# Seven block products for eight in one more token group of a channel product, on one TensorE

## The chip, the cores and the metric

The kernel runs on one NeuronCore of a Trainium2 chip. Its engines run side by side, each through its own instruction queue: TensorE (PE, matrix products, with its weight loads PEld), VectorE (DVE), ScalarE (ACT), GpSimd (POOL) and SyncE (SP, which issues DMAs). They wait for each other only on semaphores. The metric is device time in microseconds (us) of one execution, the median of several runs.

## What is computed

Three layers one after the other on 2 x 768 tokens of 384 channels: a linear-attention recurrence, a gated MLP with a product over the tokens, and an MLP mixer. The change lies in the last product pair of the mixer:

```python
def _moe2_ref(x, w_tok1, w_tok2, w_ch1, w_ch2):
    xt = x.transpose(0, 2, 1)
    h = np.maximum(xt @ w_tok1, 0.0) @ w_tok2
    u = x + h.transpose(0, 2, 1)                    # (2, 768, 384)
    h2 = np.maximum(u @ w_ch1, 0.0) @ w_ch2         # 384 -> 1536 -> 384
    return (u + h2)
```

## The kernel before

Every product of two float32 matrices is made of three products of float32r parts: each operand is split into a high part (rounded, `h`) and a low part (`l`, the rest), and `prod` issues high x high, low x high and high x low (L270, L271, L272), all added in a bank of PSUM.

The last stage, `rest`, computes `relu(u @ w_ch1) @ w_ch2`. The 1536 tokens lie in three groups g = 0, 1, 2 of 512 (two halves of 256, `ONE` and `TWO`), the 1536 hidden channels in six blocks k of 256 (`G`), the 384 input channels in three tiles of 128. A block n = (g, k) is one step of the stage.

- The first product has two forms. The plain form, `C1` (letters a and b of the order), makes 2 x 3 x 3 = 18 products of 512 columns per block; ACT takes relu and the high part from PSUM, DVE the low parts and the differences that the second product needs (`C1a`, `C1b`, letters c and d). The form `C1s` (letters g to m) takes two of the three input tiles and both halves of the tokens as a 2 x 2 block product in seven products (Strassen in Winograd's form), with the third input tile in full: 6 products of 512 columns and 21 of 256. It writes three PSUM banks x, y, z; ACT copies z (`sz`) and a part of y; DVE adds c1 and c2 (named p1, p2) from PSUM; then come relu and high part on ACT (`C1r`, o and q), the low parts (`C1l`, p and r), and the four differences `C1t` (s) on DVE.
- `C1s` needs sums of the two token halves (`sums_of_u`, E, and `split_u`, F) and of the weights (`sums_of_c1`, C, and `split_c1`, D), made on DVE, ACT and POOL in four shared tiles `st`.
- The second product, `C2` (digits 1 to 7) and `C2d` (8, 9), is the seven-product form for all groups, with right operands split by `right_split` (e, f, t, u: th on ACT, tl on DVE, L567). Its five totals per group stay in five PSUM banks for the six blocks and are added to u and stored by `finish` (G to P) and `finish_rest` (Q, S). `residual` (R) makes u from its parts on POOL.
- `z` and `Z` test whether the fast path of the recurrence was sound: two comparisons and a sum on DVE, a 1x1 product `pf` on PE, one comparison `fi` on DVE.

Before, groups 0 and 1 are in the plain form and group 2 in the form `C1s`. What runs when is written out by hand: the string `REST` has one letter for each part, and the n-th time a letter comes it does block n of its kind. Each engine works off its instructions in the order in which the string issues them. Three PSUM banks (`ps3`) serve the first product, five (`ps5`) the totals. DVE stands between nearly everything: a bank of the first product is free for the next block once DVE has read it.

Of the kernel before, what the change touches and what calls it, by code (L numbers as in the profile page):

```python
# [7 lines left out]
F32 = mybir.dt.float32  # L8
# [5 lines left out]
ALU = mybir.AluOpType  # L14
# [3 lines left out]
B, H, S, D = 2, 8, 768, 48  # L18
E = H * D
# [4 lines left out]
DCH = 1536  # L24
# [3 lines left out]
G = 2 * P  # L28
# [41 lines left out]


REST = (
# [5 lines left out]


REBIAS = 2.0 ** -112  # L80
# [5 lines left out]
class Dense:  # L86
# [442 lines left out]

    def C1(self, n, b):  # L530

        p, (g, k) = self.mm(2 * G), divmod(n, DCH // G)
        for q in range(3):
            self.prod(p, self.C1w(k, b, q), self.u[g, q], q == 0, q == 2)
        if b == 0:
            self.raw[n] = [self.temp(q) for q in ("r", "ta", "tb")]
            self.hid[n] = []
        r, h, l = self.raw[n][0], self.big("h"), self.big("l")
        act = self.nc.scalar.activation
        act(r[:, b * G:(b + 1) * G], p[:, b * G:(b + 1) * G], AF.Relu)  # L540
        act(h, p, AF.Relu)
        self.hid[n].append((h, l))
        self.raw[n].append(p)
# [68 lines left out]

    def C1l(self, n, j):
        h, l = self.hid[n][j]
        self.nc.vector.tensor_tensor(l, self.raw[n][j], h.bitcast(F32), op=ALU.subtract)

    def C1t(self, n):
        c1, c2 = self.raw[n]
# [121 lines left out]
    def rest(self, sound=None, flag=None, look=None):  # L740

        self.top.close()
        pool = lambda n, bufs: self.ctx.enter_context(self.tc.tile_pool(name=n, bufs=bufs, reuse_waits="tile"))
        self.pbig = pool("big", 8)
        self.pbig.tile([P, BPAD], F32, name="bpad", bufs=1)
        self.ptmp = pool("tmp", 6)
        self.po = pool("o", 1)
        self.banks = [self.ps3]
        self.ws, self.sw, self.raw, self.acc, self.hid, self.rests = ({} for _ in range(6))
        self.turn = False  # L750
        n = DCH // G

        later = lambda f, *a: lambda i: f(i + 2 * n, *a)
        parts = dict(A=self.sums_of_c2, B=self.split_c2, C=self.sums_of_c1, D=self.split_c1, E=lambda i: self.sums_of_u(i + 1),
                     F=lambda i: self.split_u(i + 2), a=lambda i: self.C1(i, 0), b=lambda i: self.C1(i, 1), c=self.C1a, d=self.C1b,
                     e=lambda i: self.right_split(i, 0), f=lambda i: self.right_split(i, 1),
                     o=later(self.C1r, 0), p=later(self.C1l, 0), q=later(self.C1r, 1), r=later(self.C1l, 1),
                     s=later(self.C1t), t=later(self.right_split, 0), u=later(self.right_split, 1),
                     R=self.residual, z=lambda i: flag(sound()) if sound else None, Z=lambda i: look() if look else None)
        parts.update({q: later(self.C1s, m) for m, q in enumerate("ghijklm")})  # L760
        parts.update({str(q): lambda i, q=q: self.C2(i, q) for q in range(1, 8)})
        parts.update({q: lambda i, t=t: self.C2d(i, t) for t, q in enumerate("89")})
        parts.update({q: lambda i, m=m: self.finish(i, m) for m, q in enumerate("GHIJKLMNOP")})
        parts.update({q: lambda i, t=t: self.finish_rest(i, t) for t, q in enumerate("QS")})
        count = dict.fromkeys(parts, 0)
        for part in REST.replace(" ", ""):
            parts[part](count[part])
            count[part] += 1
# [3 lines left out]
def fast(tc, ins, out, flag_pool):  # L772
    nc = tc.nc
    with ExitStack() as ctx:
# [7 lines left out]
        with ExitStack() as c1:  # L782
# [71 lines left out]
            def masked(i, o):  # L854
                A[i, o] = t = dn.a2(nm="A").rearrange("p (h c) -> p h c", c=P)
                nc.scalar.activation(t, PA[i][o], AF.Copy)  # L856
                nc.gpsimd.affine_select(out=t, in_=t, pattern=[[0, NHP], [1, P]],  # L857
                                        compare_op=ALU.is_gt, fill=0.0, base=0,
                                        channel_multiplier=-1)
# [126 lines left out]
            def ahead(f, n):  # L986
                return lambda i: f(i + n) if i + n < N else None
# [7 lines left out]
            def fetch_rest():  # L995
# [4 lines left out]
            parts = dict(  # L1000
                L=ahead(load, 2), N=ahead(load_nat, 2), F=ahead(fwd, 1), K=ahead(decay, 1),
                U=ahead(rk, 1), q=ruk, A=a0, S=scores, e=lambda i: masked(i, 0),
# [179 lines left out]
```

## Time and profile before

| | us |
|---|---|
| median of 3 runs | 381.81 (381.11 to 382.2) |
| the profiled execution | 383.05 |
| its span, first to last instruction | 381.3 |
| last stage, first channel product to last | 232.1 to 374.8 |
| mean granted TensorE clock | 0.995 of 2.4 GHz |

The profile gives busy time for each engine, the releaser of each wait (inferred from semaphore events), and single instructions with start and duration. Durations of DVE and PE instructions overlap at their ends, so a queue's pace is read from start to start. A page shows shares over the whole span; a table by windows shows them for a stage.

### The profile page before, as it was taken

The numbers are of one execution on the slowest core, as the hardware profiler recorded it, in microseconds if no ns is written. First come the engines' busy times: TensorE is split into PE (matmuls) and PEld (weight loads), VectorE is DVE, ScalarE is ACT, GpSimd is POOL, SyncE is SP. The second block draws the span as 40 slices with busy tenths as digits, with TensorE's granted clock in tenths as the row PEclk, the third lists the DMA queues.
The fourth block names the chain that finished last, engine by engine and source line by source line (L and its number), as shares of the span: only waits on it lengthen the run. The fifth ranks groups of instructions, "written<-read, shape, count | busy, mean of one in ns | idle before, by whom it ended". The sixth has DMA issues, their size and how long they took to land.

```text
span 381.3 us, 8493 instructions
## 1 busy us (share of the span) xinstructions
PE 371.1 (97%) x3287; PEld 331.3 (87%) x3287; DVE 319.2 (84%) x566; ACT 234.3 (61%) x528; POOL 195.0 (51%) x221
## 2 busy tenths in 40 slices
PE   8899999999999999999999999999999999999993
PEld 3477788889999999999999998898888888999992
DVE  6999998889888696897879687777977997799893
ACT  3599888787345896955666766545343562564650
POOL 2235468771634557768667746888714122412101
PEclk9999999999999999999999999999999999999998
DMA  8566385373343042235552340000002000011002
GB/s 242 154 217 169 110 258 156 103 212 116 95 116 147 2 124 70 83 87 159 145 164 85 124 125 0 1 2 1 2 0 69 2 14 3 0 43 42 2 2 93
DMA packets 16449, 33.72 MB, mean 88 GB/s; under 512 B 2448, under 2 KB 6544, under 8 KB 16400
## 3 DMA queue, kind: packets, MB, share of 16 engines
q1 hardware_dynamic: 15968, 32.69, 28.2%
q8 instruction: 28, 0.46, 0.5%
q10 hardware_dynamic: 432, 0.39, 0.3%
q14 instruction: 21, 0.17, 0.2%
HBM read 30.72 MB, written 2.36 MB: 87 GB/s over the span
## 4 chain that ended last, share of the span: by engine, by line
PE 88%; DVE 4%; ACT 3%; issue 1%; DMA 1%; POOL 0%; DVEq 0%; ACTq 0%
PE mm L270 26%; PE mm L272 25%; PE mm L271 25%; PE py L893 2%; PE pa L851 2%; PE py L877 1%; DVE wf L803 1%; PE mm L836 1%; PE mm L434 1%; PE tr L295 1%; PE pkv L911 1%; PE py L887 1%; DMA wf<-in_dram 1%; DVE st L230 1%; PE pt L864 1%
## 5 line engine op out<-in xcount | busy, mean ns | idle before, releaser
L232 DVE SCALAR_TENSOR_TENSOR st<-st 128x384 int32<-128x384 int32 (+1 forms) x50 | 35.3, 705 | 1.7
L857 POOL TENSOR_SCALAR_AFFINE_SELECT A<-A 128x512 f32<-128x512 f32 x24 | 18.5, 778 | 33.5 <-ACT A L856 32.0
L230 DVE SCALAR_TENSOR_TENSOR st<-st 128x384 int32<-128x384 int32 (+1 forms) x50 | 32.8, 656 | 2.3 <-ACT st L228 2.3
L540 ACT ACTIVATE r<-mm 128x256 f32<-128x256 f32 x24 | 9.2, 382 | 39.9 <-PE mm L272 39.9
L227 ACT ACTIVATE st<-st 128x384 f32<-128x384 f32 (+1 forms) x50 | 25.7, 515 | 9.9 <-DMA st<-in_dram 8.5
L228 ACT ACTIVATE st<-st 128x384 int32<-128x384 uint32 (+1 forms) x50 | 25.7, 514 | 0.0
L829 POOL TENSOR_TENSOR rk<-kr 112x512 f32<-112x512 f32 x12 | 20.0, 1666 | 10.8 <-DMA kr<-in_dram 10.8
L380 POOL TENSOR_TENSOR vs<-vs,uT 128x384 f32<-128x384 f32 x16 | 19.6, 1231 | 7.3 <-DVE vs L378 7.2
L382 ACT ACTIVATE gh<-vs 128x384 fp32r<-128x384 f32 x16 | 8.4, 524 | 24.1 <-POOL vs L380 24.1
L682 POOL TENSOR_TENSOR o<-o,part 128x256 f32<-128x256 f32 x9 | 7.1, 802 | 31.2 <-ACT part L684 23.4
L270 PE MATMUL mm<-xt,wuh 128*128 128x256 f32 x72 | 20.8, 289 | 0.0
L803 DVE TENSOR_TENSOR_SCAN wf<-wf,scan 112x516 f32<-112x516 f32 x12 | 18.6, 1554 | 2.3 <-DMA wf<-in_dram 1.8
L271 PE MATMUL mm<-xt,wuh 128*128 128x256 f32 x72 | 20.3, 282 | 0.0
L272 PE MATMUL mm<-xt,wul 128*128 128x256 f32 x72 | 20.3, 282 | 0.0
L670 POOL TENSOR_TENSOR o<-uh,ul 128x512 f32<-128x512 f32 x9 | 12.2, 1365 | 14.7 <-DVE tb L620 10.8
L546 DVE SCALAR_TENSOR_TENSOR l<-mm,h 128x512 fp32r<-128x512 f32 x24 | 16.3, 680 | 2.5 <-PE mm L271 2.5
L817 DVE TENSOR_TENSOR_SCAN wf<-wf,scan 112x516 f32<-112x516 f32 x12 | 17.9, 1489 | 0.4
L138 PE MATMUL mm<-scan 112*128 112x512 bf16 x49 | 14.1, 428 | 3.2 <-DVE scan L944 1.7
L567 DVE TENSOR_TENSOR tl<-tb,th 128x512 fp32r<-128x512 f32 x18 | 15.3, 851 | 2.2 <-ACT th L566 2.1
L825 DVE TENSOR_TENSOR kr<-kr,wf 112x1024 f32<-112x1024 f32 x12 | 15.9, 1328 | 1.2 <-DVE wf L817 0.2
L567 DVE TENSOR_TENSOR tl<-ta,th 128x512 fp32r<-128x512 f32 x18 | 16.6, 924 | 0.3 <-issue 0.3
L270 PE MATMUL mm<-woh,gh 128*128 128x384 f32 x48 | 16.2, 337 | 0.0
(298 smaller groups left out, 1487.6 us busy)
## 6 DMA issues: line engine op xcount, KB each, us to landing
st<-in_dram SPq DMA_DIRECT2D x38, 384.0 KB, 3.4
kr<-in_dram SPq DMA_DIRECT2D x12, 448.0 KB, 4.2
st<-in_dram SPq DMA_DIRECT2D x18, 256.0 KB, 4.1
wf<-in_dram SPq DMA_DIRECT2D x12, 227.5 KB, 3.0
vn<-in_dram SPq DMA_DIRECT2D x12, 192.0 KB, 4.6
out_dram<-o SPq DMA_DIRECT2D x15, 128.0 KB, 1.7
bsg<-in_dram SPq DMA_DIRECT2D x2, 192.0 KB, 3.6
out_dram<-o ACTq DMA_DIRECT2D x3, 128.0 KB, 2.1
```

What stands on the lines that cost most here:

```text
L227: nc.scalar.activation(high.bitcast(F32), high.bitcast(F32), AF.Copy, scale=REBIAS)
L228: nc.scalar.activation(low, low.bitcast(U32), AF.Copy, scale=TOP3, bias=FLOOR)
L230: nc.vector.scalar_tensor_tensor(low, high, -2 ** 31, low, op0=ALU.bitwise_and, op1=ALU.bitwise_or)
L232: nc.vector.scalar_tensor_tensor(low, high, 3, low, op0=ALU.logical_shift_left, op1=ALU.bitwise_or)
L270: mm(out, w[0], x[0], start=first, stop=False, skip_group_check=True)
L271: mm(out, w[0], x[1], start=False, stop=False, skip_group_check=True)
L272: mm(out, w[1], x[0], start=False, stop=last, skip_group_check=True)
L380: nc.gpsimd.tensor_tensor(t, t, self.uT[d, h], op=ALU.mult)
L567: self.nc.vector.tensor_tensor(lo, t, hi.bitcast(F32), op=ALU.subtract)
L803: nc.vector.tensor_tensor_scan(WF[i][:, WCOL + 2:], WF[i][:, :NHP * CW], scan1.rearrange("p h c -> p (h c)"), 0.0, op0=ALU.mult, op1=ALU.add)
L829: nc.gpsimd.tensor_tensor(RK[i][:PR], KR[i][:, 0], KR[i][:, 1], op=ALU.mult)
L857: nc.gpsimd.affine_select(out=t, in_=t, pattern=[[0, NHP], [1, P]], compare_op=ALU.is_gt, fill=0.0, base=0, channel_multiplier=-1)
```

## The change

Group 1 gets the form `C1s` too: `C1` is left for group 0, twelve blocks in place of six go through the letters g to m and o to u, and the sums E and F run twice in place of once (F four times for two). In `C1l` the low part of the second half (j = 1) is subtracted by GpSimd in place of VectorE, for groups 1 and 2. The string `REST` is new. Products, sums and results are otherwise the same.

```diff
@@ REST, first and last line
-    "abAaBc db1Azc 2e3a8A dfBeB9 cfba5d 7c64C1 2Z3857 6eA1f9 4bB23A 8Rde5a bcB796 def412 C3ac57 89f5b6 dR1A4R C23e78 "
...
-    "9KQ9NP OS")
+    "abAzcA BdeaBc Zfbd1C eAEa25 BFfD38 9c76bd 4a1F57 23e896 cA41bf B23d89 CeAacb fdAR57 641B23 89eac5 b7Rg5R dhDijf "
...
+    "Rir7js 6kl4t1 2u38mo 957q56 123p76 44rstu 12G3I5 7H6488 JLM9KQ NP9OS")
@@ C1
-        p, (g, k) = self.mm(2 * G), divmod(n, DCH // G)
+        p = self.mm(2 * G)
         for q in range(3):
-            self.prod(p, self.C1w(k, b, q), self.u[g, q], q == 0, q == 2)
+            self.prod(p, self.C1w(n, b, q), self.u[0, q], q == 0, q == 2)
@@ C1l
         h, l = self.hid[n][j]
-        self.nc.vector.tensor_tensor(l, self.raw[n][j], h.bitcast(F32), op=ALU.subtract)
+        e = self.nc.gpsimd if j == 1 else self.nc.vector
+        e.tensor_tensor(l, self.raw[n][j], h.bitcast(F32), op=ALU.subtract)
@@ rest
-        later = lambda f, *a: lambda i: f(i + 2 * n, *a)
+        later = lambda f, *a: lambda i: f(i + n, *a)
-        parts = dict(... E=lambda i: self.sums_of_u(i + 1), F=lambda i: self.split_u(i + 2), ...
+        parts = dict(... E=self.sums_of_u, F=self.split_u, ...
```

From `C1l` on, lines stand one lower in the new kernel (L615 becomes L616, L681 becomes L682).

The first place is PE at the test of the recurrence, early in the stage. h, l and c20 are operands of the second product, uh and c10 to c12 of the first. Before:

```order
L272 MATMUL mm_538_3435<-uh_488_3201,c12l_426_2824 128x512
L270 MATMUL mm_541_3449<-h_522_3380,c20h_454_3004 128x256
L271 MATMUL mm_541_3449<-l_523_3381,c20h_454_3004 128x256
L272 MATMUL mm_541_3449<-h_522_3380,c20l_455_3005 128x256
L1031 MATMUL mm_544_3465<-ones_162,okc_3463 1x1
L270 MATMUL mm_545_3470<-h_525_3394,c20h_454_3004 128x256
L271 MATMUL mm_545_3470<-l_526_3395,c20h_454_3004 128x256
```

After, on the same engine:

```order
L271 MATMUL mm_524_3384<-ul_489_3202,c12h_425_2823 128x512
L272 MATMUL mm_524_3384<-uh_488_3201,c12l_426_2824 128x512
L1032 MATMUL mm_532_3413<-ones_162,okc_3411 1x1
L270 MATMUL mm_537_3437<-uh_470_3082,c10h_313_2163 128x512
L271 MATMUL mm_537_3437<-ul_471_3083,c10h_313_2163 128x512
```

The 1x1 product has moved ahead by one block's products; behind it stood a product of the second layer, and now stands the first product of the next block.

The second place is DVE where group 0 ends (o and part are the output tiles, mm a total in PSUM). Before:

```order
L546 SCALAR_TENSOR_TENSOR l_636_3923<-mm_634_3912,h_635_3922 128x512
L567 TENSOR_TENSOR tl_638_3942<-ta_628_3897,th_637_3941 128x512
L681 TENSOR_TENSOR o_590_3686<-mm_545_3470,o_590_3686 128x256
L681 TENSOR_TENSOR o_590_3686<-mm_572_3569,o_590_3686 128x256
L681 TENSOR_TENSOR o_590_3686<-mm_545_3470,o_590_3686 128x256
L681 TENSOR_TENSOR part_591_3687<-mm_541_3449,part_591_3687 128x256
```

After:

```order
L466 TENSOR_TENSOR sw_665_4065<-f_664_4062,sw_665_4065 128x128
L577 TENSOR_TENSOR p1_658_4035<-mm_654_4031,sz_657_4034 128x512
L567 TENSOR_TENSOR tl_667_4078<-ta_660_4050,th_666_4077 128x512
L577 TENSOR_TENSOR p1_658_4035<-mm_656_4033,p1_658_4035 128x256
L682 TENSOR_TENSOR part_616_3776<-mm_548_3489,part_616_3776 128x256
L577 TENSOR_TENSOR p2_659_4036<-mm_655_4032,sz_657_4034 128x256
L682 TENSOR_TENSOR part_616_3776<-mm_569_3546,part_616_3776 128x256
L682 TENSOR_TENSOR o_615_3775<-mm_568_3542,o_615_3775 128x256
L712 TENSOR_TENSOR o_615_3775<-mm_574_3569,o_615_3775 128x256
L682 TENSOR_TENSOR o_615_3775<-mm_568_3542,o_615_3775 128x256
```

The additions that end group 0 stood behind a plain block; now they stand among the additions (L577) of a block in the new form, behind a set of weight sums (sw).

The third place is POOL from the end of group 0 on. Before:

```order
L479 TENSOR_TENSOR c22l_506_3285<-sw_621_3843,c22h_505_3284 128x128
L682 TENSOR_TENSOR o_590_3686<-o_590_3686,part_591_3687 128x256
L479 TENSOR_TENSOR s1l_575_3590<-sw_578_3595,s1h_574_3589 128x384
L479 TENSOR_TENSOR c10l_314_2164<-sw_578_3595,c10h_313_2163 128x128
L682 TENSOR_TENSOR o_590_3686<-o_590_3686,part_591_3687 128x256
```

After:

```order
L479 TENSOR_TENSOR c22l_506_3285<-sw_614_3770,c22h_505_3284 128x128
L616 TENSOR_TENSOR l_653_4011<-p2_633_3858,h_652_4010 128x512
L683 TENSOR_TENSOR o_615_3775<-o_615_3775,part_616_3776 128x256
L479 TENSOR_TENSOR s1l_550_3494<-sw_649_3965,s1h_549_3493 128x384
L479 TENSOR_TENSOR c10l_314_2164<-sw_649_3965,c10h_313_2163 128x128
L683 TENSOR_TENSOR o_615_3775<-o_615_3775,part_616_3776 128x256
L616 TENSOR_TENSOR l_669_4110<-p2_645_3950,h_668_4109 128x512
```

The new subtractions (L616) stand between the additions of the finished group (L683) and the low parts of the weight sums (L479).

## Rows read from the trace of the kernel before

**Rows 1.** The page's first part: busy us (share of the span) xinstructions.
```profile
PE 371.1 (97%) x3287; PEld 331.3 (87%) x3287; DVE 319.2 (84%) x566; ACT 234.3 (61%) x528; POOL 195.0 (51%) x221
```

**Rows 2.** By windows: the last stage, its head, a stretch of new-form blocks.
```profile
core 0: us, PE busy (x) PEld busy (x) DVE busy (x) ACT busy (x) POOL busy (x), PEclk, DMA share, GB/s
232.10:374.80 142.70, 142.66 (x903) 128.20 (x901) 120.78 (x248) 70.05 (x151) 60.96 (x74) 1.00 0.04 14
232.10:250.00 17.90, 17.90 (x88) 14.95 (x87) 12.07 (x25) 9.77 (x24) 14.10 (x21) 1.00 0.00 0
330.00:350.00 20.00, 20.00 (x152) 18.90 (x152) 19.39 (x44) 10.92 (x22) 2.18 (x3) 1.00 0.12 40
```

**Rows 3.** Timeline (start us, us, instruction): PE, and DVE's last.
```profile
232.09 0.40 PE L270 MATMUL mm<-uh,c10h 128*128 128x512 f32 x1
...
240.27 0.28 PE L270 MATMUL mm<-h,c20h 128*128 128x256 f32 x1
...
365.77 0.28 PE L270 MATMUL mm<-th,s2h 128*128 128x256 f32 x1
...
374.48 0.28 PE L272 MATMUL mm<-h,c22l 128*128 128x256 f32 x1
...
374.80 0.42 DVE L711 TENSOR_TENSOR o<-mm,o 128x256 f32<-128x256 f32 x1
```

**Rows 4.** Waits of PE's weight loads in the stage: us in total, times, longest.
```profile
PEld mm L270 <- DVE p L577: 0.4, 2, 0.2
PEld mm L270 <- DVE o L681: 0.3, 1, 0.3
```

**Rows 5.** Timeline of DVE: sums of u, a plain block, a new-form block.
```profile
299.97 1.28 DVE L513 TENSOR_TENSOR f<-uh,ul 128x512 f32<-128x512 f32 x2
...
304.29 0.42 DVE L546 SCALAR_TENSOR_TENSOR ta<-mm,r 128x256 f32<-128x256 f32 x1
...
308.23 1.40 DVE L567 TENSOR_TENSOR tl<-ta,th 128x512 fp32r<-128x512 f32 x1
...
341.69 1.28 DVE L615 TENSOR_TENSOR l<-p,h 128x512 fp32r<-128x512 f32 x2
...
344.48 0.41 DVE L681 TENSOR_TENSOR o<-mm,o 128x256 f32<-128x256 f32 x1
344.81 0.68 DVE L577 TENSOR_TENSOR p<-mm,sz 128x512 f32<-128x512 f32 x1
345.41 0.68 DVE L567 TENSOR_TENSOR tl<-ta,th 128x512 fp32r<-128x512 f32 x1
```

**Rows 6.** DVE groups by form, one line's durations, and one meeting with POOL.
```profile
L567 DVE TENSOR_TENSOR tl<-ta,th 128x512 fp32r<-128x512 f32 x18 | 16.6, 924 | 0.3 <-issue 0.3
L546 DVE SCALAR_TENSOR_TENSOR l<-mm,h 128x512 fp32r<-128x512 f32 x24 | 16.3, 680 | 2.5 <-PE mm L271 2.5
L567 DVE TENSOR_TENSOR tl<-tb,th 128x512 fp32r<-128x512 f32 x18 | 15.3, 851 | 2.2 <-ACT th L566 2.1
...
L567 DVE TENSOR_TENSOR tl<-ta,th x18: 678/688/1785, 241.9 to 369.2; 128x512 fp32r<-128x512 f32 x18
...
259.81 1.30 POOL L489 TENSOR_TENSOR f<-c22h,c22l 128x512 f32<-128x512 f32 x1
...
259.87 1.78 DVE L567 TENSOR_TENSOR tl<-ta,th 128x512 fp32r<-128x512 f32 x1
```

**Rows 7.** Timeline of PE and DVE around the 1x1 product.
```profile
240.72 0.19 PE L1031 MATMUL mm<-ones,okc 128*1 128x1 f32 x2
...
240.84 0.38 PE L270 MATMUL mm<-h,c20h 128*128 128x256 f32 x1
240.95 0.14 DVE L1032 TENSOR_SCALAR fi<-mm 1x1 int32<-1x1 f32 x1 [1.89 <-PE mm L1031]
...
241.06 0.28 PE L271 MATMUL mm<-l,c20h 128*128 128x256 f32 x1
```

**Rows 8.** Timeline of ACT and DVE where p2 is made in group 2.
```profile
326.75 0.39 ACT L598 ACTIVATE p<-mm 128x256 f32<-128x256 f32 x1 [1.63 <-PE mm L272]
...
327.16 0.42 DVE L577 TENSOR_TENSOR p<-mm,sz 128x256 f32<-128x256 f32 x1 [1.23 <-ACT p L598]
```

More of the change, by code (lines that the diff above doesn't have):

```diff
@@ L751, in rest @@
         n = DCH // G
-        later = lambda f, *a: lambda i: f(i + 2 * n, *a)
-        parts = dict(A=self.sums_of_c2, B=self.split_c2, C=self.sums_of_c1, D=self.split_c1, E=lambda i: self.sums_of_u(i + 1),
-                     F=lambda i: self.split_u(i + 2), a=lambda i: self.C1(i, 0), b=lambda i: self.C1(i, 1), c=self.C1a, d=self.C1b,
+        later = lambda f, *a: lambda i: f(i + n, *a)
+        parts = dict(A=self.sums_of_c2, B=self.split_c2, C=self.sums_of_c1, D=self.split_c1, E=self.sums_of_u,
+                     F=self.split_u, a=lambda i: self.C1(i, 0), b=lambda i: self.C1(i, 1), c=self.C1a, d=self.C1b,
                      e=lambda i: self.right_split(i, 0), f=lambda i: self.right_split(i, 1),
```

6 rows, old and new, of the table REST are left out of this document.

## The prediction

> **What bounds the kernel now.** I read the page's busy times first: TensorE (PE) is busy 97% of the span, VectorE (DVE) 84%, GpSimd (POOL) half [rows 1]. The diff touches only the last stage, so I then asked for that stage alone, from its first channel product at 232.1 us to its last at 374.8 us: PE is busy 142.66 of 142.70 us at a granted clock of 1.00, which is the 2.4 GHz level; DVE 120.78, ScalarE (ACT) 70.05, POOL 60.96 [rows 2]. The waits ahead of PE in that stretch sum to 0.7 us in three places, all of them for DVE [rows 4]. So PE's products are the length of the stage; but DVE, at 85% of it and at 19.39 of 20 us where the seven-product blocks already run, stands close behind. After the last product there is one DVE addition and a store [rows 3]; the last rows of the new order are the same (a last product, one L712 addition, one store), so the tail is taken as unchanged.
>
> **PE's saving.** A block (256 of the 1536 hidden channels, 512 tokens) in the old form is 18 products of 512 columns, in the new form 6 of 512 and 21 of 256. Products follow each other at a step that can be read from starts: 36 of 512 columns from 232.09 to 240.27 us, 0.2272 us each; 74 steps of 256 columns from 365.77 to 374.48 us, 0.1177 us each [rows 3]. Per block 12 x 0.2272 - 21 x 0.1177 = 2.726 - 2.472 = 0.25 us goes, six blocks 1.53 us. Over the whole stage the wide step comes out at 0.2290 (142.7 us less the 0.7 us of waits and less 576 x 0.1177, over 324), which gives 1.66. I take 1.6. Fewer columns by a twelfth, but 21 weight loads in place of 12: half a per cent is all there is to win.
>
> **DVE's new work.** An old block takes eight DVE instructions; one set that runs without a gap goes from 304.29 to 308.23 us, 3.94 us [rows 5]. A new block: the two low parts and the four Winograd differences, 341.69 to 344.48, 2.79; a 512-column addition out of PSUM 0.60, twice (344.81 to 345.41); a 256-column one 0.33, twice (as the one at 344.48); the two low parts of the right operand, 0.61 each by the old set: 2.79 + 1.20 + 0.66 + 1.22 = 5.87 us [rows 5], less 0.60 for the low part that POOL takes over, 5.27. Group 1: 6 x (5.27 - 3.94) = +8.0. Group 2 had the new form already and only loses its low parts: -3.6. The sums of u for group 1 and their split: 299.97 to 304.29, +4.3 [rows 5]. Sum +8.7 us, on 120.78.
>
> **POOL's new work and what it does to DVE.** Twelve subtractions of 512 columns; POOL's own rows of that size take 1.30 us [rows 6], so 15.6 us on 60.96, about 77 of 141: no bound by itself. Behind each stand the low parts of later weight sums and the additions of a finished group; PE waits for l only when C2 reads it, several products later in the new order. But the two engines disturb each other. A DVE instruction with two inputs in SBUF takes 0.678 us when it is alone and up to 1.785 us; one of the longest (259.87) covers a POOL addition at 259.81. The 24 with an input in PSUM show nothing of it, 680 ns in the mean [rows 6]. The mean lies over the median of 688 ns by 0.24 us for the 18 of one half and by 0.16 for the 18 of the other, 7.1 us in all; the other two-input lines are about half as much work again, so I put 10.6 us, an estimate, over 60.96 us of POOL work, 0.17 us a POOL microsecond. The twelve would thus cost DVE 15.6 x 0.17 = 2.7 us, between 0 (they fall beside PSUM reads) and 12 x 1.1 = 13.2 (each stops a two-input step for as long as the longest did). The Trainium skill has the rule behind this: "GPSIMD Engine Reference", Key points, says that POOL shares its SBUF interfaces with VectorE and contends with VectorE instructions that have two SBUF inputs, and that VectorE is about twice as fast at elementwise work. The trace agrees on both (1.30 against 0.60 us, and the stretch to 1.785). The rule speaks against moving the low part; by the rows the move frees 7.2 us of DVE and takes 2.7 back.
>
> DVE then has 120.8 + 8.7 + 2.7 = 132.2 us in a stage that wants to last 141.1: 94%, against 85%. ACT gains a copy of sz, one of p2 and two more passes a block; in the stretch where only new blocks run it is busy 10.92 of 20 us [rows 2], so no bound.
>
> **Where PE will wait.** Three places, from the orders in the section on the change.
> (1) The flag. PE's 1x1 product now stands directly before the next block's products, and these take the bank which fi frees on DVE; before, three short products into other banks followed. From the 1x1 product's start to the end of fi is 240.72 to 241.09, 0.37 us; a restart lost another 0.10 there, and PE already paid 0.12 for the product and that 0.10 [rows 7]. New: +0.25 us. If another bank were free it would cost nothing.
> (2) The end of group 0. In both orders PE's first product into a total of group 1 waits for DVE to have added the old total; but DVE's ten additions now stand behind a full new block and a set of weight sums, and among those of the next block. PE waits for the fifth row, counted from p2 on. From a product to the engine that reads it goes 0.23 us (as to fi [rows 7]), from ACT's copy to p2 0.41 [rows 8], five 256-column additions 5 x 0.335 = 1.68 [rows 5], a release 0.1 as above: 2.4 us after the product that the copy needs. PE has 3 + 3 + 6 + 3 + 3 = 18 products of 256 columns in between, 2.1 us. So 0.3 us late if DVE comes in time, and up to 0.65 if the POOL work there (two additions, two low parts of weights, one of the new subtractions, 4.2 us x 0.17 = 0.7) has put it back by more than it can make up. I take 0.3.
> (3) The sums of u for group 2 (4.3 us of DVE) now stand between three new blocks. From the p2 addition ahead of them to the low part that PE reads next but one, DVE has about 9.3 us of work in 9.7 us of PE. It fits with 0.4 us to spare; one collision with POOL takes up to 1.1. I take 0.2, with 0 and 0.9 as ends.
> Sum 0.75 us, between 0 and 1.8. The 0.7 us of today's waits I leave as they are; that all of them go is the lower bound's business. The sums of u for group 1 cost PE nothing early on: over 20 us of PE's products stand between them and their first reader in the new order.
>
> **The sum.** -1.6 + 0.75 = -0.85 us. The profiled execution took 383.05 us, 381.3 of it the span; it would be 382.2. Against the median of the three runs, 381.81, the forecast is **381.0 us**. Three runs lie within 1.1 us of each other, and about 0.3%, 1.1 us here, is what can be told from no change: the forecast lies inside that.
>
> **Rivals.** (a) The whole saving arrives: DVE's lag never reaches PE because operands are made well ahead (as today, where DVE at 97% costs PE nothing [rows 2, 4]). Then -1.6 to -1.2: 380.2 to 380.6 us. For it: PE lost 0.7 us in 142.7 before. Against it: the three places above, each with less than half a microsecond to spare.
> (b) DVE becomes the bound, and the kernel is slower. By the rule on the shared interface, carried to its end in this trace's rows: 13.2 us of collisions in place of 2.7 make 142.7 us of DVE work, more than PE's 141.1. At the stage's head DVE must wait for the first products (12.07 busy of 17.90 us [rows 2]); about 3 of these 5.8 idle us stay. 145.7 against 142.7 is +3.0: 384.8 us. It decides from the point where the collisions pass about 8 us, that is where DVE's work and the 3 us at the head pass 141 us. Against it: the mean stretch seen is a fifth of that.
> (c) The stage loses about what it saves, 1.2 to 2.7 us of waits: 381.4 to 382.9.
>
> **Chances.** Forecast, 380.7 to 381.4: 0.35. (a) 0.31. (c) 0.24. (b), from 383 on: 0.10. Faster by over 0.3% is (a) and a little of the forecast's lower edge, 0.34; slower by over 0.3% is (b) and a sliver of (c), 0.11; the rest, 0.55, is within 0.3%. The range of 380.0 to 382.7 leaves out most of (b) and the chance that today's waits vanish as well.
>
> **What would show it.** In the profile after: PE's products in the stage, 252 of 512 columns and 702 of 256; the gap at the 1x1 product, 0.25 us longer; the waits ahead of PE for L682 and L577 summed, 0.5 to 1.5 us more; DVE busy 130 to 135 us of the stage, the L616 rows on POOL at 1.3 us; the mean of tl at or above 0.9 us. Wrong if PE's waits stay below 0.7 us (then (a)), or if DVE shows 98% in several slices and PE gaps of a microsecond (then (b)).

## The result, and the profile after

The changed kernel takes 386.42 us (385.63 to 387.49), the kernel before on the same chip 382.0 (381.11 to 382.31). The ratio is 1.0133, 95% interval 1.0113 to 1.0153: 4.4 us slower, where the forecast was 381.0 and no difference that can be told. The range (380.0 to 382.7) missed it, and the case "slower by over 0.3%", which came, had a chance of 0.11.

The profiled execution took 385.98 us, 384.2 of it the span. The first part of its page, which answers to [rows 1]:

```profile
PE 371.7 (97%) x3341; PEld 333.2 (87%) x3341; DVE 329.3 (86%) x586; ACT 245.6 (64%) x542; POOL 213.3 (56%) x233
```

The busy shares of the whole span hardly show what happened: PE 97% as before, DVE 86% for 84%. The stage shows it. Its first product, its last one, and DVE's last addition (timeline: start us, us, instruction), as in [rows 3]:

```profile
230.68 0.40 PE L270 MATMUL mm<-uh,c10h 128*128 128x512 f32 x1
...
377.27 0.28 PE L272 MATMUL mm<-h,c22l 128*128 128x256 f32 x1
...
377.68 0.41 DVE L712 TENSOR_TENSOR o<-mm,o 128x256 f32<-128x256 f32 x1
```

From the first product to the end of DVE's last addition that is 147.4 us; before it was 143.1 (232.09 to 375.22). This length, "the stage" from here on, is read for each kernel below; it holds the 4.3 us. The stage by windows, as [rows 2], with the stretch that loses most:

```profile
core 0: us, PE busy (x) PEld busy (x) DVE busy (x) ACT busy (x) POOL busy (x), PEclk, DMA share, GB/s
230.68:377.80 147.12, 143.57 (x957) 129.99 (x955) 133.11 (x269) 81.17 (x165) 78.09 (x86) 1.00 0.04 14
302.00:353.00 51.00, 48.08 (x328) 43.33 (x327) 46.92 (x90) 28.34 (x54) 17.76 (x15) 1.00 0.06 19
```

The same stretch of 51 us in the kernel before:

```profile
302.00:353.00 51.00, 51.00 (x348) 46.86 (x348) 45.30 (x93) 27.58 (x57) 14.33 (x14) 1.00 0.06 19
```

Before, PE is busy for 51.00 of 51 us with DVE at 45.30. After, by busy time, PE stands for 2.9 of them; from start to start, as counted below, its steps there are 5.4 us too long. DVE does not look full, 46.92 of 51; but set against what PE did in that time it is 46.92 us of DVE for 48.08 of PE, 98%, where it was 45.30 for 51.00, 89%. The granted clock is 1.00 throughout, the 2.4 GHz level, so nothing of it is the clock's.

The waits ahead of PE's weight loads in the stage (us in total, times, longest), for [rows 4]:

```profile
PEld mm L271 <- DVE tl L567: 1.9, 4, 0.6
PEld mm L270 <- DVE p L577: 1.5, 4, 0.7
PEld mm L270 <- ACT th L566: 0.9, 1, 0.9
PEld mm L271 <- DVE utl L524: 0.6, 1, 0.6
PEld mm L1032 <- issue: 0.4, 1, 0.4
PEld mm L270 <- DVE fi L1033: 0.3, 1, 0.3
PEld mm L270 <- DVE o L682: 0.3, 1, 0.3
```

5.9 us in many small pieces, where it was 0.7 in three. The one put down to ACT goes back to DVE as well: before its th, ACT had stood 2.21 us for DVE's ta (L621). Added up from start to start, with the undisturbed step of each width taken off, PE's steps in the stage are 6.7 us too long after and 0.7 before, 6.0 us more. The stage grew by 4.3, so the products themselves took 1.7 us less: their saving arrived, and the waits ate it more than three times over.

How one of them comes about, between GpSimd, DVE and PE (timeline of all engines):

```profile
320.54 1.31 POOL L671 TENSOR_TENSOR o<-uh,ul 128x512 f32<-128x512 f32 x1 [2.20 <-DMA out_dram<-o]
320.62 1.52 DVE L621 TENSOR_TENSOR tb<-p,tb 128x256 f32<-128x256 f32 x1
322.06 0.68 DVE L524 TENSOR_TENSOR utl<-tb,uth 128x512 fp32r<-128x512 f32 x1
322.10 0.28 PE L270 MATMUL mm<-uth,s1h 128*128 128x256 f32 x1
...
322.80 0.39 PE L271 MATMUL mm<-utl,s1h 128*128 128x256 f32 x1 [0.41 <-DVE utl L524]
```

A residual addition starts on GpSimd 0.08 us before a small DVE subtraction with two inputs in SBUF; that takes 1.52 us where its like takes 0.42. Such a meeting of the two engines shows as a longer duration and not as a wait: no semaphore stands between them, so for these two the sentence of the first section, that engines wait for each other only on semaphores, does not hold. utl, behind it on DVE, comes 1.1 us later, and PE's second product of a group waits for it: 0.70 us from start to start in place of 0.12.

### The profile page after: what moved, and what is told of

The parts are those of the page before. It is cut to its first block, busy times and chain, and to the rows that moved or that the text cites. A ratio compares the mean times of both kernels' runs of the same rounds, so it can differ in the third digit from the quotient of the medians.

```text
span 384.2 us, 8688 instructions
## 1 busy us (share of the span) xinstructions
PE 371.7 (97%) x3341; PEld 333.2 (87%) x3341; DVE 329.3 (86%) x586; ACT 245.6 (64%) x542; POOL 213.3 (56%) x233
## 4 chain that ended last, share of the span: by engine, by line
PE 73%; DVE 14%; ACT 6%; issue 3%; POOL 2%; DMA 1%; SPq 0%; DVEq 0%; ACTq 0%; POOLq 0%
PE mm L270 21%; PE mm L271 20%; PE mm L272 20%; DVE p L577 3%; PE py L894 2%; PE pa L852 2%; DVE tb L621 2%; DVE ta L621 2%; DVE tl L567 2%; PE py L878 1%; DMA kr<-in_dram 1%; PE mm L837 1%; PE mm L434 1%; DVE l L616 1%; PE tr L295 1%
## 5 line engine op out<-in xcount | busy, mean ns | idle before, releaser
L616 POOL TENSOR_TENSOR l<-p,h 128x512 fp32r<-128x512 f32 x12 | 15.8, 1319 | 41.7 <-ACT h L610 32.3
L610 ACT ACTIVATE h<-p 128x512 fp32r<-128x512 f32 x24 | 15.2, 633 | 7.6 <-PE mm L271 7.0
L804 DVE TENSOR_TENSOR_SCAN wf<-wf,scan 112x516 f32<-112x516 f32 x12 | 17.6, 1463 | 2.1 <-DMA wf<-in_dram 1.5
L818 DVE TENSOR_TENSOR_SCAN wf<-wf,scan 112x516 f32<-112x516 f32 x12 | 16.7, 1395 | 0.4
L566 ACT ACTIVATE th<-ta 128x512 fp32r<-128x512 f32 x18 | 11.3, 629 | 8.6 <-DVE ta L621 5.9
L272 PE MATMUL mm<-woh,gl 128*128 128x384 f32 x48 | 16.1, 336 | 0.0
L577 DVE TENSOR_TENSOR p<-mm,p 128x256 f32<-128x256 f32 (+1 forms) x24 | 13.3, 556 | 3.2 <-PE mm L272 1.5
L271 PE MATMUL mm<-wol,gh 128*128 128x384 f32 x48 | 16.1, 335 | 0.0
```

The lines of the kernel that those rows point to most:

```text
L271: mm(out, w[0], x[1], start=False, stop=False, skip_group_check=True)
L272: mm(out, w[1], x[0], start=False, stop=last, skip_group_check=True)
L577: add = lambda o, i, j: self.nc.vector.tensor_tensor(o, i, j, op=ALU.add)
L616: e.tensor_tensor(l, self.raw[n][j], h.bitcast(F32), op=ALU.subtract)
```

## The experiments

At the start stood three theories for the 6 us. **C**, collisions: DVE's two-input instructions are stretched by GpSimd's work, and DVE has no room to take it up. **W**, work: the amount that DVE has to do is too much. **Q**, queue: GpSimd's own queue delivers late. All kernels are the changed one with one edit, unless it is said that they are the one before.

| run | edit | us | ratio to before (95%) | stage, us |
|---|---|---|---|---|
| before | | 381.7 to 382.0 | 1 | 143.1 |
| after | | 386.42 | 1.0113 to 1.0153 | 147.4 |
| e1 | all low parts on DVE | 392.75 | 1.0251 to 1.0355 | 153.3 |
| e2 | moved low parts left out | 386.84 | 1.0103 to 1.0179 | 147.6 |
| e3 | residual by DMA | 382.62 | 1.0007 to 1.0039 | 145.1 |
| e4 | e2 and e3 | 383.16 | 1.0011 to 1.0058 | 144.4 |
| e5 | residual earlier | 388.20 | 1.0155 to 1.0189 | 148.0 |
| e6 | sums of u of group 2 left out | 384.35 | 1.0039 to 1.0090 | 144.9 |
| e7 | e3, additions back into a scratch tile | 385.49 | 1.0070 to 1.0114 | 147.7 |
| e8 | before, low part moved alone | 385.40 | 1.0079 to 1.0112 | 147.1 |
| e9 | before, residual by DMA | 380.28 | 0.9954 to 0.9980 | 142.8 |
| e11 | another order | 386.30 | 1.0114 to 1.0159 | 143.5, flag apart |
| e12 | that order, mended | 386.60 | 1.0109 to 1.0156 | 147.7 |
| e13 | e12, residual by DMA | 381.91 | 0.9995 to 1.0023 | 144.4 |

The stage is that of the profiled execution alone. It starts between 230.6 and 232.4 us in these executions although nothing ahead of it was changed, so a whole time carries up to 1.8 us that belongs to no edit; where the two columns differ, the stage is what the argument goes by. The profiled execution of e3 was a longer one than its others (388.83 us, first product at 235.81), so of it only the stage is used (granted clock 1.00 from 235 to 381 us). The stage of e8 holds 1.5 us that is the clock's (last section).

### The low parts back on DVE, and left out (e1, e2)

```diff
# e1: as before
-        e = self.nc.gpsimd if j == 1 else self.nc.vector
+        e = self.nc.vector
# e2
+        if j == 1:
+            self.hid[n][j] = h, h
+            return
```

> The changed kernel with one edit undone: all low parts of C1l on VectorE again, none on GpSimd. Two theories of the +4.4 us. Theory C (collisions): GpSimd instructions each stop a VectorE instruction with two SBUF inputs for up to 1.1 us, and in the second half of the stage, where VectorE has no slack, that reaches TensorE. Theory W (amount of work): VectorE is late because of the 8.7 us of new work of its own, wherever GpSimd's work is. C: VectorE gets 12 x 0.60 = 7.2 us more but loses the 3.9 us by which the moved subtractions stretch it, so about even with the changed kernel, 384.5 to 387 us. W: 7.2 us more on an engine that is already late, 389 to 392 us.

> The changed kernel with the twelve moved subtractions left out altogether: the high part stands in for the low part as an operand of the second product (that part of the computation is left out). VectorE's own work is that of the changed kernel. C: the 3.9 us of stretch by these twelve go, and most of it lies where TensorE waits: 382.5 to 384.5 us. W: nothing changes for VectorE, 386 to 387 us.

e1 took 392.75 us, the stage 5.9 us longer than after. Its window:

```profile
231.00:383.00 152.00, 143.50 (x954) 129.78 (x953) 139.57 (x279) 81.34 (x165) 62.15 (x73) 1.00 0.04 12
```

DVE had 139.6 us of work in it in place of 133.1, and the time went up by nearly as much as the work did, to a little above W's range. So at this load DVE's work sets the pace, and the move to GpSimd is what kept the change from being worse: in this order it gains 6.3 us.

In e2 the twelve subtractions are nowhere. C wanted 382.5 to 384.5, W 386 to 387; it took 386.84, nothing gained, as W said. That speaks against collisions as a cause, but at the place shown above for after the trace has this (timeline, GpSimd, DVE, PE):

```profile
320.87 4.48 POOL L673 TENSOR_TENSOR o<-uh,ul 128x512 f32<-128x512 f32 x3 [14.36 <-DMA out_dram<-o]
...
320.95 1.51 DVE L623 TENSOR_TENSOR tb<-p,tb 128x256 f32<-128x256 f32 x1
322.39 1.79 DVE L524 TENSOR_TENSOR utl<-tb,uth 128x512 fp32r<-128x512 f32 x1
...
324.23 0.39 PE L271 MATMUL mm<-utl,s1h 128*128 128x256 f32 x1 [1.52 <-DVE utl L524]
```

With the moved subtraction gone from between them, the three residual additions of group 1 run in one row of 4.48 us. They now meet tb and utl as well, and PE waits 1.5 us here where it waited 0.4. What the twelve gave back in other places, the additions took here. Work that is left out on GpSimd moves all that stands behind it: over the whole stage DVE's instructions still stand 12.1 us over their undisturbed time, where it was 13.7 with the twelve. That nothing at all was gained is shown; that this trade is the whole reason is not.

### The residual additions (e3, e4, e7)

```diff
# e3
-        self.nc.gpsimd.tensor_tensor(o, hi.bitcast(F32), lo.bitcast(F32), op=ALU.add)
+        self.nc.sync.dma_start(o, hi.bitcast(F32))
# e7: e3, and behind the DMA
+        self.nc.gpsimd.tensor_tensor(self.whole[:, :2 * G], hi.bitcast(F32), lo.bitcast(F32), op=ALU.add)
```

> The changed kernel with the nine additions of residual (GpSimd, 512 columns, 13.4 us in all) replaced by DMA copies of u's high part; the low part of u in the residual is left out. The twelve moved subtractions stay. C: 3.5 us of stretch of VectorE by these nine go: 383 to 385 us. W: 386 to 387 us. If only the moved subtractions matter, it stays at 386 as well.

> Both edits of the last two runs together: neither the moved subtractions nor the residual additions on GpSimd (the low part of one operand and of u in the residual are left out). C: what remains in the second half on GpSimd are short additions and low parts of weights: 380.5 to 382.5 us, TensorE's bound of 380.4 nearly reached. W: 386 to 387 us.

> The kernel of e3 (the residual by a DMA copy of the high part, 382.6 us) with the nine GpSimd additions put back at the same places of the order, of the same operands and size, but writing a scratch part of another tile that nobody reads: GpSimd works and meets DVE as before, but does not wait for the stores and nobody waits for its result. Theory C (the additions cost by meeting DVE's two-input instructions): back to 385.5 to 387. Theory Q (they cost because GpSimd's queue waits there for the stores of the group before, and later low parts stand behind that): stays at 382.3 to 383.3.

e3 took 382.62 us, 3.8 less than after and just below C's range, with nine GpSimd instructions gone of the 86 in the stage. At the same place of the program (timeline):

```profile
326.29 0.43 DVE L621 TENSOR_TENSOR tb<-p,tb 128x256 f32<-128x256 f32 x1
326.63 0.69 DVE L524 TENSOR_TENSOR utl<-tb,uth 128x512 fp32r<-128x512 f32 x1
...
327.91 0.28 PE L271 MATMUL mm<-utl,s1h 128*128 128x256 f32 x1
```

tb is back at 0.43 us, utl is begun 1.28 us before PE's product that reads it, and no wait stands there. e4, without the moved subtractions too, gains nothing in time over e3 (383.16 against 382.62) and misses C's range of 380.5 to 382.5. In its stage DVE stands only 7.3 us over its undisturbed time, less than the 11.2 of the kernel before, and still PE's waits sum to 3.4 us, where it was 0.7: so a part of the loss needs no meeting with the moved subtractions or the additions. What is left for it is DVE's own new work, its order, and the other work on GpSimd; these runs don't part them.

e7 tells C from Q: the nine additions are back, of the same operands and size, but their result is read by nobody and they don't wait for stores. It took 385.49 us with a stage of 147.7: all of what e3 had won in the stage is lost again (in the longest of its four executions, 387.39), and 2.9 of its 3.8 us in the medians. So it is neither their wait for the stores nor a reader that costs; they cost by being at work beside DVE. Timeline:

```profile
320.69 1.69 POOL L673 TENSOR_TENSOR part<-uh,ul 128x512 f32<-128x512 f32 x1 [0.39 <-DVE o L684]
...
321.46 1.20 DVE L621 TENSOR_TENSOR ta<-p 128x256 f32<-128x256 f32 x1
```

That GpSimd's queue is not waited for can also be read in after: DVE waits 0.5 us in all for it in the stage, ACT 0.7, PE not at all.

### The sums of u, and the additions at another place (e6, e5)

```diff
# e6, in sums_of_u and split_u
+        if n:
+            return
...
+        if n > 1:
+            self.u[2, 3 + n % 2] = self.u[1, 3 + n % 2]
+            return
# e5: REST, R and M some letters earlier
-    ... 57os1O p23htq 89ijrk l6D412 53mgCh "
-    "u8so7D pij9t6 412qk3 lm8rug 5Eso76 ptF9qh ir41jM u23k8l 59sF7g 6mtuR1 2hijko p348qr R5l79m g6hsij otRkq4 ...
+    ... 57os1O pM23ht q89ijr kl6RD4 1253Rm "
+    "gChu8s Ro7Dpi j9t641 2qk3lm 8rug5E so76pt F9qhir 41ju23 k8l59s F7g6mt u12hij kop348 qr5l79 mg6hsi jotkq4 ...
```

> The changed kernel with the sums of u for group 2 (four subtractions, two additions, two low parts on DVE, two high parts on ScalarE) left out; group 2 uses those of group 1 in their place. It leaves out 4.3 us of DVE work at about 310 to 320 us, and nothing else. Theory W (DVE's amount of work from 300 us on sets the end): 4.3 us of DVE were worth 3.8 us elsewhere, so 382.3 to 383.5. Theory C (the loss comes from GpSimd's residual additions, which stretch DVE's two-input instructions; the sums only add lag at one place, where the next waits take it up): 385.0 to 386.3. My prediction's own price of this place, 0.2 us (0 to 0.9), would give 385.5 to 386.4.

> The changed kernel (386.4 us) with one thing moved and nothing left out: the last store of group 0 is issued earlier (M directly behind O), so that the three residual additions of group 1 can run on GpSimd between the blocks at about 300 to 310 us, where DVE is busy 8.26 of 10 us, in place of 320 to 330 us, where it has no room. Theory P (a meeting of the residual additions with DVE costs only where DVE is late already): 2 of the 3.8 us that went with all nine additions come back, 383.5 to 385.0. Theory A (a meeting puts DVE behind wherever it falls, because the lag is carried on to the next place where TensorE waits): 386 to 387. If the additions now hold up a low part that the next block needs, 387 to 389.

e6 took 384.35 us, 2.1 less than after, the stage 2.5 us less, for 4.3 us of DVE work: between the two theories. Its executions lie far apart, 382.83 to 385.46, and the stage is that of the longest. The prediction had priced this work at 0.2 us of waits, at most 0.9.

In e5 the three additions stand some 20 us earlier, where DVE had idle time. It took 388.20, slower than after. The waits at 320 to 340 us did go, but new ones came earlier: 1.47 us for an addition p (L577) at 312.89, and nearly as long a one on GpSimd's own queue (timeline; s1m is the low part of a weight sum):

```profile
301.77 1.31 POOL L671 TENSOR_TENSOR o<-uh,ul 128x512 f32<-128x512 f32 x1
303.04 1.18 POOL L479 TENSOR_TENSOR s1m<-sw,s1m 128x384 fp32r<-128x384 f32 x1
...
304.27 0.39 PE L272 MATMUL mm<-uth,s1m 128*128 128x256 f32 x1 [1.40 <-POOL s1m L479]
```

The addition holds up the low part behind it, and PE waits 1.4 us for that. Theory P, that a better place is enough, was not borne out here.

### One part alone, on the kernel before (e8, e9)

```diff
# e8: the kernel before
-        self.nc.vector.tensor_tensor(l, self.raw[n][j], h.bitcast(F32), op=ALU.subtract)
+        e = self.nc.gpsimd if j == 1 else self.nc.vector
+        e.tensor_tensor(l, self.raw[n][j], h.bitcast(F32), op=ALU.subtract)
# e9: the kernel before, with the edit of e3
```

> The kernel before (381.8 us) with one part of the change alone: the second low part on GpSimd, which there is six subtractions of group 2. DVE has 3.6 us less work of its own, GpSimd 7.7 us more. If DVE had been holding TensorE at the three places that sum to 0.7 us: 381.1 to 381.5. If the move gives back in meetings what it frees, as leaving the moved subtractions out showed: 381.6 to 382.1. If the low parts come too late on GpSimd or meet DVE in the tight stretch at 330 to 350 us: 382.3 to 383.5.

> The kernel before (381.7 us) with its nine residual additions of GpSimd replaced by a DMA copy of the high part of u; the low part of u in the residual is left out. Theory C (a residual addition costs 1.1 us of DVE for each meeting, and that reaches TensorE only where DVE has no slack): before, TensorE waits only 0.7 us in the stage, so 381.2 to 381.8. If DVE's stretched instructions already cost here what they cost in the changed kernel (3.8 us for nine): 378 to 380.

e8 has six subtractions moved and nothing else, and is 3.7 us slower than before, above all three ranges that were expected. DVE's own work fell by 3.6 us, yet its instructions that stand over their undisturbed time (0.69, 0.43 and 0.29 us by size) by more than 0.15 us lost 18.8 us in place of 11.2. Near the end of the stage (timeline, GpSimd, DVE, PE):

```profile
359.94 1.41 POOL L616 TENSOR_TENSOR l<-p,h 128x512 fp32r<-128x512 f32 x1 [2.36 <-ACT h L610]
...
360.12 1.78 DVE L616 TENSOR_TENSOR l<-p,h 128x512 fp32r<-128x512 f32 x1
...
361.31 1.76 POOL L671 TENSOR_TENSOR o<-uh,ul 128x512 f32<-128x512 f32 x1
...
361.82 1.80 DVE L567 TENSOR_TENSOR tl<-ta,th 128x512 fp32r<-128x512 f32 x1
363.54 0.68 DVE L577 TENSOR_TENSOR p<-mm,sz 128x512 f32<-128x512 f32 x1
...
363.99 0.28 PE L272 MATMUL mm<-h,c21l 128*128 128x256 f32 x1
...
365.72 0.41 DVE L577 TENSOR_TENSOR p<-mm,p 128x256 f32<-128x256 f32 x1
...
366.19 0.39 PE L270 MATMUL mm<-uth,s1m 128*128 128x256 f32 x1 [1.93 <-DVE p L577]
```

The kernel before has here two low parts in a row and then tl:

```profile
359.07 1.28 DVE L615 TENSOR_TENSOR l<-p,h 128x512 fp32r<-128x512 f32 x2
360.27 0.69 DVE L567 TENSOR_TENSOR tl<-ta,th 128x512 fp32r<-128x512 f32 x1
```

From start to the next instruction's start the three took 1.81 us; now two take 3.42, one stretched by the moved subtraction and the next by the residual addition, which the subtraction has pushed into it. The addition p, on which PE's bank depends, comes late by it, and PE stands 1.9 us. So the move saves DVE 0.6 us a piece and can cost it 1.1 in one meeting, and then a second by what it moves on GpSimd. In the profiled execution (387.06) 2.7 us of the stage's 4.0 are new waits of PE for p, and 1.5 us are the clock's (last section); how much of the clock's part is in the other executions, whose median is the 3.7, the runs don't show.

e9 took 380.28 us, 1.6 less than before, which lies between its two expectations, but its stage is only 0.4 shorter (142.8 against 143.1). In the profiled executions the stage of e9 begins 1.5 us earlier (230.61 against 232.09), ahead of all that the edit touches; whether the other 1.2 us of the medians lie there, stays open. The same nine that cost the changed kernel 2.3 us of its stage cost the kernel before 0.4: DVE has room there.

### Another order (e11, e12, e13)

```diff
# e12: REST, from the middle of the stage
-    "u8so7D pij9t6 412qk3 lm8rug 5Eso76 ptF9qh ir41jM u23k8l 59sF7g 6mtuR1 2hijko p348qr R5l79m g6hsij otRkq4 1rlmuG "
+    "Chm8oD ij9t61 2qpk3l m8rug5 4EsFo7 6pt9qh ir419j uM23k8 l5Fs7g 6m1tR2 hijop3 ku4R8q rl79mg 6ohsij t5qRpk 41rlmG "
# e13: e12 with the edit of e3
```

> The changed kernel (386.4 us) in full, nothing left out, with another order of the letters of the stage: between the blocks of groups 1 and 2 the residual additions, the end of each group, the low parts and the relu of a block each stand a few letters earlier or later, so that GpSimd's work falls beside other DVE work and each bank is read earlier. DVE's and GpSimd's amount of work is the same. Theory P (the loss is made by where the work stands: about 6 us of waits in 302 to 353 us, of which the order can give back most): 381 to 383.5. Theory W (132 us of DVE work in a stage of 141 us is too much in any order): 385 to 387.5.

> The changed kernel (386.4 us) in full, with nothing left out or exchanged, in an order of letters built on that of e11: the flag stands where the changed kernel has it (0.3 us in place of e11's 2.8), and in the three blocks where e11 exchanged operands (in block 0 the second low part, in block 5 the right split, in block 6 the order of the two halves) the letters stand in their proper order again; some letters of the end of group 0 and of groups 1 and 2 are shifted once more by one to five places. e11's stage without its 2.8 us at the flag was 143.5 us, against 143.1 before and 147.4 in the changed kernel. Theory P (the loss is made by where the work stands): 381.3 to 383.3, no slower than before by more than its runs scatter. Theory W (the amount of DVE work is too much in any order): 385 to 387.

> The kernel of e12 with the nine residual additions of GpSimd replaced by a DMA copy of the high part of u (the low part of u in the residual is left out), as in e3 and e9. If the saving of TensorE's products, 1.6 us in the stage, arrives where neither meetings with the additions nor the order stand in its way: 1.2 to 1.6 us below e9 (the kernel before with the same replacement, 380.3), so 378.6 to 379.3. If DVE's load still takes the saving: 380.3 to 382.

In e11 operands of three blocks had changed places (e12's text names them); number and size of the instructions are those of the full kernel. It took 386.30 us, in W's range, but its stage, counted behind the flag, is 143.5, about that of before. In its order the flag is the first letter, and PE waits for it at the very start (timeline):

```profile
231.58 0.40 PE L272 MATMUL mm<-t2h,hl 128*128 128x512 f32 x1
234.61 0.19 PE L1032 MATMUL mm<-ones,okc 128*1 128x1 f32 x2 [2.63 <-DVE okc L1027]
```

That seemed to promise 383 with the flag put back. But while PE stood, DVE worked on, from 232.2 to 234.5 us at low parts and comparisons that fall inside the stage of the other kernels, and with exchanged operands the waits of three blocks are not those of the full kernel: the 143.5 can't be set against the others. e12 took 386.60, in W's range again, with a stage of 147.7. Its letters differ from e11's in some places, and with them the moments at which GpSimd and DVE meet: over the stage DVE's instructions stand 19.9 us over their undisturbed time, where it was 13.7 in after. PE's two longest waits, 0.96 and 1.38 us for additions p (L577), lie at the end of group 0 (285.64 and 294.00 us). Behind them the three residual additions of group 1 stretch three of DVE's instructions in 8 us, and PE waits twice more (0.51 and 0.71 us). Timeline, two of the three and the second wait:

```profile
323.21 2.76 POOL L671 TENSOR_TENSOR o<-uh,ul 128x512 f32<-128x512 f32 x2 [2.80 <-DMA out_dram<-o]
...
323.28 1.52 DVE L621 TENSOR_TENSOR tb<-p,tb 128x256 f32<-128x256 f32 x1
...
328.92 1.79 DVE L567 TENSOR_TENSOR tl<-tb,th 128x512 fp32r<-128x512 f32 x1
...
330.76 0.39 PE L271 MATMUL mm<-tl,s2m 128*128 128x256 f32 x1 [0.71 <-DVE tl L567]
```

So of three full orders (after, e5, e12) none is under 386 us. Theory P is not refuted by that, but no order that was run bears it out: moving letters chooses which instructions meet, and each choice here found new ones.

e13 took 381.91 us: in this order, too, the nine additions are worth 3.3 us of the stage and 4.7 in all. It is still 1.6 us above e9, which has the same replacement in the kernel before. So even with that relief the change doesn't give PE's 1.6 us; its stage of 144.4 us has 3.8 us of waits, the longest 1.8 us for an addition p at the end of group 0. No version with seven products in group 1 was faster than its counterpart without.

## Why the prediction was wrong, step by step

**PE's saving: right.** -1.6 us was forecast; 4.3 us of stage against 6.0 us more waits leave -1.7.

**DVE's work: right.** 132.2 us were forecast; the window shows 133.11, for 120.78 in [rows 2].

**The size of the collisions: right in sum, wrong in the lines.** 2.7 us more were forecast; by the instructions that stand over their time by more than 0.15 us it is 13.7 against 11.2, +2.5, and 6.0 against 3.9 of it between 302 and 353 us. The lines say that the sum agrees in part by luck. The mean of tl was to be at or above 0.9 us, as in [rows 6]; it fell, and the stretch went to the low parts and the differences (L621). DVE by form, with one line of GpSimd:

```profile
L567 DVE TENSOR_TENSOR tl<-ta,th 128x512 fp32r<-128x512 f32 x18 | 14.4, 802 | 0.0
L567 DVE TENSOR_TENSOR tl<-tb,th 128x512 fp32r<-128x512 f32 x18 | 14.0, 780 | 1.1 <-ACT th L566 1.0
L616 DVE TENSOR_TENSOR l<-p,h 128x512 fp32r<-128x512 f32 x12 | 9.1, 755 | 0.0
L621 DVE TENSOR_TENSOR tb<-p,tb 128x256 f32<-128x256 f32 x12 | 7.3, 609 | 0.4
...
L616 POOL TENSOR_TENSOR l<-p,h 128x512 fp32r<-128x512 f32 x12 | 15.8, 1319 | 41.7 <-ACT h L610 32.3
```

GpSimd's 15.8 us for the twelve were forecast as 15.6. The Trainium skill ("GPSIMD Engine Reference", Key points) names the shared interface and the instructions that suffer, those with two inputs in SBUF; the rows agree in kind, from 0.42 to 1.52 us for tb.

**Place 1, the flag: right.** +0.25 us forecast. PE's 1x1 product starts at 234.88, the next at 235.30, with a wait of 0.3 us for fi in the list above; the steps there are 0.3 us too long.

**Place 2, the end of group 0: right in size, but no new loss.** 0.3 us forecast; the list shows 0.3 for o L682, and [rows 4] had the same 0.3 for o L681 already. The forecast counted it as new.

**Place 3, the sums of u: the step that failed.** "It fits with 0.4 us to spare; one collision with POOL takes up to 1.1. I take 0.2, with 0 and 0.9 as ends." Without that work the stage is 2.5 us shorter and the median 2.1 (e6), more than the upper end. The term was priced as one place, met by one collision, with DVE on time at its start and free behind it. It is not one place. From 302 to 353 us DVE is busy, its meetings included, 0.98 us for each microsecond of PE, so a lag made there is hardly made up before the next product that needs DVE, and further meetings become waits of PE: nine of 0.2 to 0.9 us in that stretch. The sum of waits came out at 0.75 us (0 to 1.8), and 6.0 were added: 2.5 of them go with the work of this place, and most of the rest fell at places that the prediction had not named.

**The measure behind it.** The forecast took DVE's share over the whole stage, 94%, as the room that it has. Set against PE's busy time in the same stretch, DVE's was 90% from 250 to 302 us of the new profile (46.47 to 51.85), where old and new blocks mix, and 98% from 302 to 353, where only new ones run: the mean of a stage hides the stretch that decides. The row for 330 to 350 us in [rows 2], DVE 19.39 of 20 with PE never waiting, was taken as a sign that DVE at 97% costs nothing. It held for those 20 us; in the 51 us around them the kernel before had 89%.

This ratio is a warning and no threshold. DVE's busy time holds the meetings, and PE's falls by its own waits, so both ends of it move when the loss comes. Two other stretches of 51 us, from e13 and from e6:

```profile
294.00:345.00 51.00, 51.00 (x362) 47.52 (x361) 48.26 (x104) 31.77 (x61) 17.56 (x16) 1.00 0.12 42
309.00:360.00 51.00, 49.72 (x357) 46.06 (x357) 42.76 (x84) 28.09 (x53) 20.01 (x16) 1.00 0.06 19
```

In the first 95% cost nothing, in the second PE stood 1.3 us at 86%: where in the stretch DVE comes late counts too, and not its share alone.

**The rivals.** Rival (b) was right in its mechanism, DVE as the bound by way of the shared interface, and 1.6 us short of the time (384.8 against 386.4). Its price was wrong, and so its chance of 0.10: it was made to need 8 us of collisions over the stage, because it asked when DVE's sum passes PE's sum. 2.5 us more of them were enough, since what counts is the stretch in which DVE has no room, and that they fall there. Rival (c), 1.2 to 2.7 us of waits, was the same thing too small. Rival (a) took the 0.7 us of [rows 4] as proof of room.

What the runs leave open: how the 4.3 us divide between DVE's own work and the meetings. The two are not separate amounts: 6.5 us more work cost 5.9 us of stage (e1), 4.3 us less gave 2.5 (e6), nine additions fewer 2.3 (e3) and twelve moved subtractions fewer nothing (e2). With both left out 3.4 us of waits remain (e4), so the meetings with these two are not all of it.

## What to carry to other kernels

Before an engine beside the bound one is given more work, set its busy time against the bound engine's in the stretch that gets the work, not over the stage: here the stage's mean was forecast at 94%, and in the 51 us that decided it went from 89% to 98% and PE stood for 2.9 us. No share that is safe came out of these runs (86% cost 1.3 us in e6, 95% nothing in e13). Moving an instruction with two SBUF inputs from VectorE to GpSimd frees its time on VectorE, but takes up to 1.1 us back in one meeting with a VectorE instruction of the same kind; here it paid where VectorE would otherwise have been the bound (6.3 us between e1 and after) and cost where it was not (3.7 us in e8). And a GpSimd addition that nobody waits for is not free when VectorE is full: nine of them cost 2.3 us of stage in one kernel and 0.4 in another.

## What the runs showed of the hardware

What a meeting costs does not depend on the size of the VectorE instruction: 0.42 us became up to 1.52 (256 columns), 0.69 up to 1.78 to 1.80 (512 columns), beside GpSimd instructions of 1.3 to 1.8 us. It depends on how much of the GpSimd instruction is left. In the lines above tb begins 0.08 us behind an addition and ends 0.29 us after it (after), ta begins 0.77 us behind one and ends 0.28 us after it (e7), l and tl of 512 columns end 0.55 us after theirs (e8). In all fourteen traces 500 of VectorE's additions and subtractions with two inputs outside PSUM stand over their undisturbed time by more than 0.15 us, and each of them began while a GpSimd instruction was running. Where only one such instruction was met (208 of them), the end came 0.15, 0.28, 0.41 or 0.55 us after GpSimd's, for 128, 256, 384 or 512 columns, within 0.02 us. So VectorE's instruction makes nearly no headway until GpSimd's is over, and pays for the rest of it: 1.1 us when it begins right behind an addition of 1.3, little when it begins near its end (0.49 us in the mean over the 28 in the stage of after). Small VectorE instructions lose most in proportion. Those with an input in PSUM show nothing of it: of 1636 that ran beside a GpSimd instruction none took over 0.07 us longer.

GpSimd is stretched as well when it comes second: the residual addition in e8 begins at 361.31 us while VectorE's l runs until 361.90, and takes 1.76 us in place of 1.30. The mean over the nine in after is 1.50.

In e8's profiled execution PE stood from 364.3 to 366.2 us, and then the granted clock, which had been 1.00 (2.4 GHz), went to 0.50 (1.2 GHz); the window:

```profile
367.00:370.00 3.00, 3.00 (x16) 3.00 (x15) 2.78 (x6) 2.40 (x5) 0.00 (x0) 0.50 0.00 0
```

Sixteen products of 256 columns follow each other there at 0.21 us in place of 0.118, 1.5 us lost after the wait was over. In e11's profiled execution PE stood 2.6 us at 231.9 and the clock stayed at 1.00. Why the one and not the other, these runs don't show.
